# Attention, token routing and expert layers on one core: later weight loads, one engine for the bf16 copies, a new order for the attention part

## The chip, the core and the metric

One core of a Trainium2 chip runs the whole program. The metric is the device time of one execution in microseconds (us), lower is better; the median of several runs is quoted. The engines are PE (TensorE matmul; PEld is its weight load), DVE (VectorE), ACT (ScalarE), POOL (GpSimd) and SP (SyncE, which here only issues DMAs). Each engine runs its own instructions in the order in which they were written, and waits on semaphores for the others.

## The reference

Two stages. The first is a decaying linear attention over q, k, v of shape (4 batches, 8 heads, 768 positions, 64 channels); the second gives each of the 3072 tokens to one of 8 experts, 384 tokens to each, by a greedy pass over the sorted gate logits, and runs the expert's two matmuls.

```python
intra = np.einsum('bhic,bhjc->bhij', qb, kb) * Dmask[None]
intra = np.einsum('bhij,bhjd->bhid', intra, vb)
inter = np.einsum('bhid,bhde->bhie', qb * lam_pow[None], kv_state)
out[:, :, sl] = intra + inter
...
logits = x @ w_gate
order = np.argsort(-flat)
...
h = np.maximum(x[mask] @ w1[e], 0.0)
out[mask] = h @ w2[e]
```

## The kernel before

**Attention** works in 24 groups of 128 positions (6 per batch, all 8 heads together). A group is a chain of about thirty named steps, listed in `_Attn.OPS` with an engine, a planned duration and the steps that they follow. For group g:

- SP loads q, k and v (`ldq`, `ldk`, `ldv`, L1092, 256 KB each, in rows of 256 bytes) into tiles of a pool with seven buffers per name, so that the load of group g waits until group g-7 has been used up.
- POOL or DVE splits k into a high and a low half in place (`klo`, L1098, tile kf); POOL scales v (`vs`, L1113), ACT rounds it (`vh`), POOL takes the rest (`vl`, L1124).
- PE turns q and k (L1129), forms the scores S (L1166); ACT copies them out (`sph`, L1173), DVE takes the low half (`spl`, L1179), POOL zeroes what lies above the diagonal (`mk`, the mask, L1183, tile sp), and PE multiplies with v (`in0`, `in1`, L1206) and with the running state (`inter`, L1194). `state`, `sth`, `stl` carry the state on.
- DVE scales the result (`xs`, L1215). `xb` (L1224 on ACT, L1226 on DVE) makes a bf16 copy, in one of four buffers, and SP stores it to x_dram (`stx`, L1229). PE, ACT and DVE turn and split x (`Tx`, `xh`, `xl`, L1243) and form the gate logits (`gate`, `lg`, L1256).

**Routing and experts.** When all logits are there, DVE and PE rank them (L156 to L404). Pieces of that ranking for the first groups, and constants that POOL makes with iotas (L50, L39), are planned into the last part of the attention. Then POOL gathers the tokens of an expert from x_dram (L657), PE runs the two matmuls (L688, L701), POOL scatters the rows out (L707). The sixteen weight tensors (w1 and w2 of eight experts, 2 MB of f32 read and 1 MB of bf16 written each) are loaded by DMAs that POOL issues (`load_w`, L639, tile w): nine are planned into the attention part (the steps `lw`), seven follow among the gathers.

**What sets the order.** `_Plan.emit` plays all steps through once, with the planned durations and a fixed latency per engine, and always takes the step that can begin first; among those within 0.05 us of each other the lowest number `OFF[name] + g * PERIOD` wins. The kernel is then written out in that order, engine by engine. The plan leaves no wait behind: at run time an engine waits only for the data or the buffer that an instruction needs. A weight load in the attention part needs neither, so POOL issues it as soon as it comes to it in its queue.

Of the kernel before, what the change touches and what calls it, by code (L numbers as in the profile page):

```python
# [17 lines left out]
ACT = mybir.ActivationFunctionType  # L18
# [790 lines left out]
def _check_and_mend(ctx, tc, L, router, moe, dram, fi):  # L809
    fv = tc.nc.values_load(fi, min_val=0, max_val=1)  # L810
    moe.free = False
    with tc.If(fv > 0):
        with ExitStack() as fctx:
            _exact_path(fctx, tc, L, router, moe, dram)
# [225 lines left out]
class _Attn:  # L1040

    PERIOD = 4.65
    OFF = dict(S=54.69, Tk=24.2, Tq=49.21, Tx=-82.61, gate=99.21, in0=35.81, in1=1.68, inter=74.69, kT=111.17, klo=26.02, ldk=11.31, ldq=7.1, ldv=7.57, lg=-21.29, mk=-54.22, qh=-5.75, ql=31.77, sph=96.51, spl=-4.24, state=12.87, sth=69.68, stl=10.78, stx=59.94, vh=-1.2, vl=94.76, vs=-6.84, xb=69.71, xh=15.09, xl=21.76, xs=38.18)

    def __init__(self, ctx, tc, q, k, v, lam, w_gate, identf, logits, x_dram):
        nc = tc.nc
# [230 lines left out]
    def stl(self, g):  # L1277
# [5 lines left out]
        ("ldq", "SP", 1.16, None, "Tq-7"),  # L1283
        ("ldk", "SP", 1.16, None, "state-7 Tk-7"),
        ("ldv", "SP", 1.16, None, "vs-7"),
        ("klo", "Pool", 1.18, None, "ldk"),
        ("vs", "Pool", 1.10, None, "ldv vl-2"),
        ("vh", "ACT", 0.64, None, "vs state-4 in0-4 in1-4"),
        ("vl", "Pool", 1.18, None, "vh state-4 in0-4 in1-4"),
        ("Tq", "PE", 0.42, None, "ldq ql-1"),  # L1290
        ("qh", "ACT", 0.60, None, "Tq S-3 inter-3"),
        ("ql", "DVE", 0.69, None, "qh S-3 inter-3"),
# [1 line left out]
        ("kT", "ACT", 0.62, None, "Tk S-2"),  # L1294
        ("S", "PE", 0.68, None, "kT ql spl-1"),
        ("sph", "ACT", 1.02, None, "S in0-2 in1-2"),
        ("spl", "DVE", 1.22, None, "sph"),
        ("mk", "Pool", 1.35, None, "spl"),
# [14 lines left out]
    )  # L1313

    def engine(self, name, g, eng, dur):
        if name == "xb":
            return (("ACT", 0.63), ("DVE", 0.40))[g % 2]
        if name == "klo" and g % 3 == 2:
            return "DVE", 0.78
        return eng, dur  # L1320

    def plan(self, plan, extra):
# [8 lines left out]
        for g in range(24):  # L1331
            for name, eng, dur, when, deps in self.OPS:
# [12 lines left out]
                if name in ("klo", "xb"):  # L1345
                    f = lambda g, f=f, eng=eng: f(g, getattr(self.nc, en[eng]))
                plan.op(name, g, eng, dur, lambda f=f, g=g: f(g), dd + extra.get((name, g), []),
                        self.OFF[name] + g * self.PERIOD)


@with_exitstack
def kernel(
    ctx: ExitStack,
    tc: tile.TileContext,
    q: bass.AP,
    k: bass.AP,
    v: bass.AP,
    lam: bass.AP,
    moe_w_gate: bass.AP,
    moe_w1: bass.AP,  # L1360
    moe_w2: bass.AP,
    out: bass.AP,
):
    nc = tc.nc
    P = 128
    E = mybir.EngineType
    const = ctx.enter_context(tc.tile_pool(name="const", bufs=1))
    dram = ctx.enter_context(tc.tile_pool(name="dram", bufs=1, space=bass.MemoryType.DRAM))
    identf = const.tile([P, P], F32, name="identf")
    identb = const.tile([P, P], BF16, name="identb")  # L1370
    logits = const.tile([P, 24, 8], F32, name="logits")
    x_dram = dram.tile([3072, 512], BF16, name="x_dram")
    router = _Router(ctx, tc, identf, identb)
    moe = _Moe(ctx, tc, identb, x_dram, moe_w1, moe_w2, out, 10)
    with ExitStack() as actx, tc.manual_schedule(
            engines={E.PE, E.Pool, E.DVE, E.Activation, E.SP}):
        attn = _Attn(actx, tc, q, k, v, lam, moe_w_gate, identf, logits, x_dram)
        attn.consts()
        plan = _Plan()
        extra = {}  # L1380
        router.plan(plan, attn, logits, extra)
        for m in range(9):
            plan.op("lw", m, "Pool", 0.9, lambda m=m: moe.load_w(m),
                    [("mk", min(15 + m, 23)), ("lw", m - 1)], 0)
        attn.plan(plan, extra)
        plan.emit()
    moe.open(ctx)
    fi = _route_and_moe(ctx, tc, logits, router, moe, range(9, 16))
    _check_and_mend(ctx, tc, logits, router, moe, dram, fi)
# [31 lines left out]
```

## Time and profile before

| | |
|---|---|
| median of 3 runs | 310.71 us (307.69 to 315.24) |
| the profiled execution's own time | 310.75 us |
| its span, first to last instruction | 308.9 us |
| mean granted clock of PE | 0.895 of full speed |
| busy, share of the span | PE 78%, DVE 60%, ACT 49%, POOL 57% |
| HBM read and written | 55.60 MB and 9.44 MB |

The span is 1.85 us shorter than the execution's own time; what lies around it is not seen by the profile. A share of busy time is a mean over stages that have different limits, so the prediction reads stages. In the rows below a time begins with the start in us from the beginning of the span, then the duration; a bracket at the end is the idle time of the engine before the instruction and what ended it. In a row of the stages stand, after the stretch and its length, the busy us of PE, PEld, DVE, ACT and POOL (with the number of instructions), the granted PE clock, the busy share of the 16 DMA engines (which can go a little over 1) and what they moved in GB/s. In a row by lines stand the count, the busy us and the mean ns of one, and the idle time before.

### The profile page before, as it was taken

The page shows a single profiled execution, that of the slowest core. Times are in us where ns is not written, and L with a number is a line of the kernel's source. Part 1 is how long each engine was busy: PE and PEld are TensorE (multiplying, and loading weights), DVE is VectorE, ACT ScalarE, POOL GpSimd, SP SyncE. Part 2 cuts the span into 40 slices and gives each one's busy share as a digit, 9 for nine tenths or more (in the row PEclk, how much of TensorE's full clock was granted, in tenths as well). Part 3 has the DMA queues.
Part 4 walks back from the last instruction along what each step waited for, and adds up shares of the span by engine and source line. Part 5 has one row for each costly group of instructions (what it writes and reads, how often), then busy time and mean ns, then how long its engine had stood idle before and what let it go on. Part 6 is the DMA issues. An engine that isn't in the chain of part 4 may idle for free.

```text
span 308.9 us, 8631 instructions
## 1 busy us (share of the span) xinstructions
PE 240.8 (78%) x3512; PEld 193.7 (63%) x3525; DVE 185.7 (60%) x560; ACT 151.3 (49%) x261; POOL 177.4 (57%) x184
## 2 busy tenths in 40 slices
PE   1698988898998149985339986999787999799980
PEld 0678976787897048874237784666455676567750
DVE  0479997979999147999974756577854770000000
ACT  4489776768885226852000001444334445456650
POOL 1799979698993088989650064854262246334220
PEclk9999999979999758997555685899999999999997
DMA  7998998999999969999930019899996113212111
GB/s 138 219 217 181 202 206 195 227 231 233 224 217 175 217 143 165 219 215 222 218 61 0 2 52 145 154 211 227 243 228 243 71 68 114 104 61 102 70 72 40
DMA packets 94671, 48.90 MB, mean 158 GB/s; under 512 B 76960, under 2 KB 88224, under 8 KB 94624
## 3 DMA queue, kind: packets, MB, share of 16 engines
q0 software_dynamic: 15616, 26.22, 40.3%
q1 hardware_dynamic: 79008, 22.05, 34.8%
q8 instruction: 30, 0.49, 0.7%
q14 instruction: 17, 0.14, 0.2%
HBM read 55.60 MB, written 9.44 MB: 211 GB/s over the span
## 4 chain that ended last, share of the span: by engine, by line
PE 30%; DVE 17%; issue 17%; DMA 14%; POOL 13%; ACT 4%; SPq 1%; POOLq 0%; ACTq 0%; DVEq 0%
DMA out_dram<-oe,perm 6%; PE p L688 5%; DMA w<-in_moe_w_dram 4%; PE p L701 4%; DVE sp L1179 4%; PE spare L272 4%; PE S L1166 3%; POOL sp L1183 3%; PE XL L1206 2%; POOL out_dram L707 2%; PE stp L1267 2%; POOL kf L1098 2%; DVE xb L1226 2%; PE KT L1129 2%; POOL vs L1113 2%
## 5 line engine op out<-in xcount | busy, mean ns | idle before, releaser
L688 PE MATMUL p<-xeT,w 128*128 128x256 bf16 (+1 forms) x512 | 50.1, 252 | 6.8 <-ACT xeT L675 2.4
L688 PEld LDWEIGHTS <-w 128*128 128x128 bf16 x512 | 40.5, 100 | 15.4 <-issue 8.6
L707 POOL DMA_INDIRECT out_dram<-oe,perm x24 | 24.0, 999 | 43.6 <-ACT oe L706 32.8
L657 POOL DMA_INDIRECT xe<-x_dram,perm x24 | 25.4, 1058 | 40.6 <-DVE B L387 20.7
L701 PE MATMUL p<-w,hT 128*128 128x512 bf16 x179 | 43.7, 379 | 0.8
L693 ACT ACTIVATE hT<-p 128x512 bf16<-128x512 f32 (+1 forms) x64 | 30.9, 492 | 19.5 <-PE p L688 13.7
L675 ACT COPY xeT<-pt 128x1024 bf16<-128x1024 bf16 (+1 forms) x16 | 12.8, 800 | 43.4 <-PE pt L671 41.0
L1179 DVE TENSOR_TENSOR sp<-S,sp 128x1024 f16<-128x1024 f32 x24 | 31.9, 1330 | 2.8 <-ACT sp L1173 2.4
L1183 POOL TENSOR_SCALAR_AFFINE_SELECT sp<-sp 128x1024 f32<-128x1024 f32 x24 | 27.0, 1127 | 7.6 <-DVE sp L1179 6.9
L1113 POOL TENSOR_TENSOR vs<-vf,lamneg 128x512 f32<-128x512 f32 x24 | 27.5, 1149 | 6.2 <-DMA vf<-in_v_dram 6.1
L1124 POOL TENSOR_TENSOR vl<-vs,vh 128x512 bf16<-128x512 f32 x24 | 28.2, 1182 | 2.1 <-ACT vh L1119 2.1
L706 ACT COPY oe<-p 128x512 f32<-128x512 f32 x24 | 14.0, 588 | 31.1 <-PE p L701 21.2
L1173 ACT ACTIVATE sp<-S 128x1024 f32<-128x1024 f32 x24 | 24.7, 1030 | 7.9 <-PE S L1166 7.0
L701 PEld LDWEIGHTS <-hT 128*128 128x128 bf16 x192 | 17.0, 97 | 17.9 <-issue 1.8
L1098 POOL TENSOR_TENSOR kf<-kf 128x512 f16<-128x512 f32 x16 | 17.0, 1064 | 17.9 <-DMA kf<-in_k_dram 17.9
L1206 PE MATMUL XL<-vh,sp 128*128 128x64 bf16 x384 | 23.5, 199 | 1.6 <-POOL sp L1183 0.8
L1166 PE MATMUL S<-qh,kT 64*128 64x128 f16 x384 | 21.1, 221 | 4.4 <-DVE sp L1179 4.1
L1267 PE MATMUL stp<-vl,kf 128*128 128x128 bf16 x80 | 16.0, 232 | 10.9 <-POOL vl L1124 10.9
L1129 PE MATMUL QT<-identf,qf 128*128 128x128 f32 x96 | 16.6, 299 | 9.3 <-DMA qf<-in_q_dram 5.0
L1206 PEld LDWEIGHTS <-sp 128*128 128x128 bf16 (+1 forms) x576 | 21.8, 102 | 2.9 <-POOL sp L1183 2.2
L1267 PEld LDWEIGHTS <-kf 128*128 128x128 bf16 (+1 forms) x240 | 16.1, 105 | 11.8 <-issue 11.0
L1166 PEld LDWEIGHTS <-kT 64*128 64x128 bf16 (+1 forms) x576 | 17.5, 96 | 7.9 <-issue 6.9
(255 smaller groups left out, 569.6 us busy)
## 6 DMA issues: line engine op xcount, KB each, us to landing
w<-in_moe_w_dram POOLq DMA_DIRECT2D x16, 1024.0 KB
qf<-in_q_dram SPq DMA_DIRECT2D x24, 256.0 KB, 5.2
kf<-in_k_dram SPq DMA_DIRECT2D x24, 256.0 KB, 4.8
vf<-in_v_dram SPq DMA_DIRECT2D x24, 256.0 KB, 5.4
x_dram<-xb SPq DMA_DIRECT2D x24, 128.0 KB, 4.7
xe<-x_dram,perm POOLq DMA_INDIRECT x24
out_dram<-oe,perm POOLq DMA_INDIRECT x24
lam_sb<-in_lam_dram SPq DMA_DIRECT2D x1, 4.0 KB, 2.9
```

What stands on the lines that cost most here:

```text
L657: nc.gpsimd.indirect_dma_start(out=xe[:, c, :], out_offset=None, in_=self.x_dram, in_offset=bass.IndirectOffsetOnAxis(ap=pm, axis=0), boun ...
L688: nc.tensor.matmul(p1[:, f, 0:n, :], self.w1t[e][:, kc, fc * P : (fc + 1) * P], j["xeT"][:, kc, 0:n, :], start=(kc == 0), stop=(kc == 3), ...
L693: nc.scalar.activation(hT[:, fp, :, 0:n, :], p1[:, :, 0:n, :], ACT.Relu)
L701: nc.tensor.matmul(p2, j["hT"][:, kc // 2, kc % 2, c, :], self.w2t[e][:, kc, :], start=(kc == 0), stop=(kc == 7))
L707: sc = nc.gpsimd.indirect_dma_start(out=self.out, out_offset=bass.IndirectOffsetOnAxis(ap=j["perms"][c], axis=0), in_=oe, in_offset=None, ...
L1113: self.nc.gpsimd.tensor_tensor(d["vs"], d["v"], self.lamneg[:, g % 6, :, None].to_broadcast([128, 8, 64]), OP.mult)
L1124: self.nc.gpsimd.tensor_tensor(d["vl"], d["vs"], d["vh"], OP.subtract)
L1166: self.nc.tensor.matmul(S[:, a, hp, :], kk[r, hp, :], qq[r, hp, :], start=(i == 0), stop=(i == 2))
L1179: self.nc.vector.tensor_tensor(lo, d["S"].rearrange("p a c i -> p (a c i)"), hi, OP.subtract)
L1183: self.nc.gpsimd.affine_select(out=sf, in_=sf, compare_op=OP.is_ge, fill=0.0, base=0, pattern=[[0, 8], [1, 128]], channel_multiplier=-1)
L1206: self.nc.tensor.matmul(d["XL"][:, a, hp, :], ss[:, a, hp, :], vv[:, 2 * hp + a, :], start=(first and hp == 0 and i == 0), stop=(i == 2), ...
L1267: self.nc.tensor.matmul(self.stp[:, hp, :], kk[:, hp, :], vv[:, hs, :].rearrange("p h d -> p (h d)"), start=(g % 6 == 0 and hp == 0 and i ...
```

## The change

Four things are changed.

1. A weight load in the plan now follows the last loads of q, k and v (group 23) as well as the mask 15 + m.
2. All 24 bf16 copies `xb` are on ACT; before, the 12 odd groups were on DVE.
3. DVE keeps `klo` of groups 4, 9, 14 and 19; before, it had groups 2, 5, 8, 11, 14, 17, 20 and 23. POOL so has 20 of the 24 instead of 16.
4. Planned durations of five steps are set anew, and the table `OFF` is another one.

```diff
@@ class _Attn
-    OFF = dict(S=54.69, Tk=24.2, Tq=49.21, Tx=-82.61, gate=99.21, in0=35.81, in1=1.68, inter=74.69, kT=111.17, klo=26.02, ldk=11.31, ldq=7.1, ldv=7.57, lg=-21.29, mk=-54.22, qh=-5.75, ql=31.77, sph=96.51, spl=-4.24, state=12.87, sth=69.68, stl=10.78, stx=59.94, vh=-1.2, vl=94.76, vs=-6.84, xb=69.71, xh=15.09, xl=21.76, xs=38.18)
+    OFF = dict(S=38.76, Tk=-14.89, Tq=147.97, Tx=-2.41, gate=2.43, in0=170.45, in1=-148.02, inter=-167.53, kT=141.1, klo=52.88, ldk=36.69, ldq=34.47, ldv=38.97, lg=-259.14, mk=-45.12, qh=27.26, ql=58.61, sph=117.65, spl=65.52, state=205.19, sth=37.97, stl=-17.43, stx=-83.47, vh=74.3, vl=-25.62, vs=110.96, xb=281.9, xh=-1.86, xl=-37.54, xs=47.27)
...
-        ("klo", "Pool", 1.18, None, "ldk"),
+        ("klo", "Pool", 1.06, None, "ldk"),
...
-        ("vl", "Pool", 1.18, None, "vh state-4 in0-4 in1-4"),
+        ("vl", "Pool", 1.17, None, "vh state-4 in0-4 in1-4"),
...
-        ("spl", "DVE", 1.22, None, "sph"),
-        ("mk", "Pool", 1.35, None, "spl"),
+        ("spl", "DVE", 1.33, None, "sph"),
+        ("mk", "Pool", 1.12, None, "spl"),
...
-        ("xb", None, 0.63, None, "xs stx-4"),
+        ("xb", "ACT", 0.62, None, "xs stx-4"),
...
     def engine(self, name, g, eng, dur):
-        if name == "xb":
-            return (("ACT", 0.63), ("DVE", 0.40))[g % 2]
-        if name == "klo" and g % 3 == 2:
-            return "DVE", 0.78
+        if name == "klo" and g % 5 == 4:
+            return "DVE", 0.95
         return eng, dur
...
-                    [("mk", min(15 + m, 23)), ("lw", m - 1)], 0)
+                    [("ldq", 23), ("ldk", 23), ("ldv", 23), ("mk", 15 + m), ("lw", m - 1)], 0)
```

POOL's queue around its first weight loads, before (kf is `klo`, sp the mask, w a weight load; the mask behind w_0_70 is that of group 16, the `klo` behind w_0_71 that of group 22):

```order
L1113 TENSOR_TENSOR vs<-vf,lamneg 128x512
L639 DMA w_0_70<-in_moe_w_dram 128x4x1024
L1183 AFFINE_SELECT sp<-sp 128x1024
L1098 TENSOR_TENSOR kf<-kf 128x512
L639 DMA w_0_71<-in_moe_w_dram 128x8x512
L1098 TENSOR_TENSOR kf<-kf 128x512
L1124 TENSOR_TENSOR vl<-vs,vh 128x512 x2
L1183 AFFINE_SELECT sp<-sp 128x1024
```

The same place after (the first `klo` is group 22's, the second group 23's; the first mask is group 17's):

```order
L1098 TENSOR_TENSOR kf<-kf 128x512
L1183 AFFINE_SELECT sp<-sp 128x1024
L1124 TENSOR_TENSOR vl<-vs,vh 128x512
L639 DMA w_0_70<-in_moe_w_dram 128x4x1024
L1098 TENSOR_TENSOR kf<-kf 128x512
L639 DMA w_0_71<-in_moe_w_dram 128x8x512
L1183 AFFINE_SELECT sp<-sp 128x1024
L639 DMA w_1_72<-in_moe_w_dram 128x4x1024
L1113 TENSOR_TENSOR vs<-vf,lamneg 128x512
L639 DMA w_1_73<-in_moe_w_dram 128x8x512
L1183 AFFINE_SELECT sp<-sp 128x1024
```

The first weight load has moved from behind mask 15 to behind mask 17 and `klo` 22; only `klo` 23 stands behind it, and the loads follow each other more closely.

SP's queue near its end, before (group 22's last two loads, then those of group 23 and stores of x):

```order
L1092 DMA vf<-in_v_dram 128x8x64
L1229 DMA x_dram<-xb 128x512
L1092 DMA kf<-in_k_dram 128x8x64
L1092 DMA qf<-in_q_dram 128x8x64
L1092 DMA vf<-in_v_dram 128x8x64
L1229 DMA x_dram<-xb 128x512
L1092 DMA kf<-in_k_dram 128x8x64
L1229 DMA x_dram<-xb 128x512 x11
```

The same queue after, around its only run of three stores (the loads ahead are q and k of group 17):

```order
L1092 DMA qf<-in_q_dram 128x8x64
L1092 DMA kf<-in_k_dram 128x8x64
L1229 DMA x_dram<-xb 128x512 x3
L1092 DMA vf<-in_v_dram 128x8x64
L1092 DMA qf<-in_q_dram 128x8x64
L1092 DMA kf<-in_k_dram 128x8x64
```

Thirteen stores stand ahead of the last load in both programs; before, they come one to a group from group 11 on, after, they stand earlier and less evenly, the first behind sixteen loads.

DVE's queue at the end of the attention, before (L1179 is `spl` of group 23; L178 to L188 are pieces of the ranking):

```order
L1179 TENSOR_TENSOR sp<-S,sp 128x1024
L178 TENSOR_SCALAR dg<-identf,m_3305 3x3
L1226 CAST xb<-xs 128x512
L1243 TENSOR_TENSOR xl<-XT,xh 128x512
L1215 TENSOR_TENSOR xs<-XL,lampow 128x2x4x64
L1256 TENSOR_REDUCE logits<-XT 128x8
L1280 TENSOR_TENSOR stl<-stp,sth 128x512
L185 COPY mb<-mb_ps 128x3
L1226 CAST xb<-xs 128x512
L188 TENSOR_SCALAR rg<-mb 128x2
```

The same place after:

```order
L178 TENSOR_SCALAR dg<-identf,m_3333 3x3
L1179 TENSOR_TENSOR sp<-S,sp 128x1024
L1243 TENSOR_TENSOR xl<-XT,xh 128x512
L1215 TENSOR_TENSOR xs<-XL,lampow 128x2x4x64
L1256 TENSOR_REDUCE logits<-XT 128x8
L1280 TENSOR_TENSOR stl<-stp,sth 128x512
L185 COPY mb<-mb_ps 128x3
L188 TENSOR_SCALAR rg<-mb 128x2
L191 SCALAR_TENSOR_TENSOR lo<-rg,mb 128x2
```

The copies are gone from DVE, and the ranking's small steps stand directly behind the attention's. From the gathers on, the order of every engine is the same in both programs.

## Rows read from the trace of the kernel before

**Rows 1.** Busy time by stages, core 0.

```profile
65.00:92.00 27.00, 25.25 (x573) 23.41 (x572) 24.77 (x40) 22.66 (x38) 25.01 (x23) 0.98 1.04 225
92.00:112.00 20.00, 8.28 (x189) 6.89 (x187) 8.79 (x15) 7.39 (x13) 6.14 (x7) 0.80 1.11 206
112.00:139.00 27.00, 23.93 (x510) 21.76 (x510) 23.86 (x38) 17.89 (x30) 23.86 (x24) 0.90 0.98 176
139.00:152.00 13.00, 6.07 (x90) 5.06 (x86) 12.63 (x32) 2.30 (x4) 10.63 (x20) 0.72 1.18 219
152.00:180.00 28.00, 21.11 (x174) 16.52 (x174) 18.36 (x75) 0.00 (x0) 6.72 (x9) 0.58 0.19 37
```

**Rows 2.** POOL in order of time: masks, weight load, `klo`, iotas, first gather.

```profile
42.04 1.09 POOL L1183 TENSOR_SCALAR_AFFINE_SELECT sp<-sp 128x1024 f32<-128x1024 f32 x1 [0.69 <-DVE logits L1256]
...
50.28 1.08 POOL L1183 TENSOR_SCALAR_AFFINE_SELECT sp<-sp 128x1024 f32<-128x1024 f32 x1
...
71.03 1.09 POOL L1183 TENSOR_SCALAR_AFFINE_SELECT sp<-sp 128x1024 f32<-128x1024 f32 x1 [1.56 <-DVE sp L1179]
...
91.34 1.00 POOL L639 DMA_DIRECT2D w<-in_moe_w_dram  x1
92.87 1.09 POOL L1183 TENSOR_SCALAR_AFFINE_SELECT sp<-sp 128x1024 f32<-128x1024 f32 x1 [0.53 <-DVE sp L1179]
...
109.18 1.03 POOL L1098 TENSOR_TENSOR kf<-kf 128x512 f16<-128x512 f32 x1 [13.33 <-DMA kf<-in_k_dram]
...
112.39 1.08 POOL L1183 TENSOR_SCALAR_AFFINE_SELECT sp<-sp 128x1024 f32<-128x1024 f32 x1
...
138.49 1.09 POOL L1183 TENSOR_SCALAR_AFFINE_SELECT sp<-sp 128x1024 f32<-128x1024 f32 x1
...
141.18 3.58 POOL L50 IOTA i_kt<- 128x768 bf16 x4
...
179.77 1.60 POOL L657 DMA_INDIRECT xe<-x_dram,perm  x1 [20.70 <-DVE B L387]
```

**Rows 3.** SP's last loads in order of time, and how long loads took to land.

```profile
93.63 0.46 SPq L1092 DMA_DIRECT2D kf<-in_k_dram  x1
94.14 8.11 SPq L1092 DMA_DIRECT2D qf<-in_q_dram  x1
...
108.86 0.39 SPq L1092 DMA_DIRECT2D kf<-in_k_dram  x1
...
DMA to landing us min/median/max: 3.6/5.2/16.1
```

**Rows 4.** DMA queues from 88 to 110 us: packets, MB, share of 16 engines.

```profile
q1 hardware_dynamic: 8373, 2.38, 57.7%
q0 software_dynamic: 1568, 2.10, 55.3%
```

**Rows 5.** DVE in order of time at the end of the attention.

```profile
138.06 1.54 DVE L178 TENSOR_SCALAR dg<-identf,m 3x3 f32<-3x3 f32 x1
...
141.86 3.99 DVE L1226 CAST xb<-xs 128x512 bf16<-128x512 f32 x1
...
148.44 1.43 DVE L1226 CAST xb<-xs 128x512 bf16<-128x512 f32 x1
...
151.52 0.17 DVE L1256 TENSOR_REDUCE logits<-XT 128x8 f32<-128x16 f32 x1 [0.15 <-PE XT L1252]
```

**Rows 6.** Groups of instructions by line: copies, v's scaling, `klo`, weight loads.

```profile
L1113 POOL TENSOR_TENSOR vs<-vf,lamneg 128x512 f32<-128x512 f32 x24 | 27.5, 1149 | 6.2 <-DMA vf<-in_v_dram 6.1
...
L1098 POOL TENSOR_TENSOR kf<-kf 128x512 f16<-128x512 f32 x16 | 17.0, 1064 | 17.9 <-DMA kf<-in_k_dram 17.9
...
L639 POOL DMA_DIRECT2D w<-in_moe_w_dram x16 | 14.2, 891 | 2.9 <-DMA w<-in_moe_w_dram 2.9
...
L1226 DVE CAST xb<-xs 128x512 bf16<-128x512 f32 x12 | 13.4, 1116 | 0.0
...
L1224 ACT CAST xb<-xs 128x512 bf16<-128x512 f32 x12 | 7.5, 623 | 11.9 <-issue 7.0 <-DMA x_dram<-xb 3.3 <-DVE xs L1215 1.7
```

## The prediction

> **What bounds the kernel now.** I read the stages first, then POOL in order of time, then what SP and the DMA queues did where POOL stood still.
>
> The stages [rows 1] show a hole. From 65 to 92 us PE, DVE and POOL are each busy for about 25 of 27 us, and the DMA engines move 225 GB/s: everything is near its limit at once. From 92 to 112 us no engine is busy for half of the time, but the DMA share is 1.11. The DMAs work, and not on what the engines wait for.
>
> POOL in order of time [rows 2] says where. The masks of groups 11 and 16 start at 71.03 and 92.87, five groups apart, so a group takes 4.37 us. The next mask, group 17's, starts at 112.39, 19.52 us later. Just before, at 91.34, POOL issued the first weight load; then `klo` of group 22 waited 13.33 us for its k. That k had been issued at 93.63 [rows 3], so it took over 15 us to land where the median load takes 5.2; the issue of the next q alone held SP for 8.11 us, and the last k went out only at 108.86. Between 88 and 110 us the two queues had nearly equal shares of the DMA engines, 55.3% for the weights and 57.7% for loads and stores [rows 4]. Two weight tensors, not needed before the gathers at 179.77 [rows 2], took half of the service from the last few loads, needed at once.
>
> By the Trainium skill, page "DMA: Bandwidth & Descriptors", section "Queues, rings and completion order", each DMA engine takes turns between the queues that have work, a packet at a time. The nearly equal shares agree with that.
>
> The second place is the end of the attention. From the last mask at 138.49 [rows 2] to the last logits at 151.52 [rows 5] 13.03 us pass, DVE is busy for 12.63 of 13 us [rows 1], and two bf16 copies take 3.99 and 1.43 us there [rows 5], while POOL runs its iotas from 141.18 [rows 2].
>
> **The change part by part.** The sum is made against the profiled execution, 310.75 us, which is the median of the runs shown (310.71) for all purposes.
>
> *Weight loads later: -15.2.* In the new order the first weight load stands behind mask 17 and `klo` 22. When POOL reaches it, k of group 22 has landed, and of 72 loads only the last few can be in flight. If the pitch of 4.37 holds for one more group, mask 17 starts at 92.87 + 4.37 = 97.24 instead of 112.39: 15.15 us. What is late next is the pitch itself. It can't fall far: up to k of group 22 there are 68 loads of 262 kB and 12 stores of 131 kB, 19.4 MB, at 225 GB/s 86 us; with some 2 us of start, 5.2 for landing and 1.06 for `klo` [rows 6] mask 17 can't start before about 94.5, a further 2.7 at best. On the other side, the old order once lost a group's time to such waiting: masks at 42.04 and 50.28 are 8.24 apart, 3.87 over the pitch. Two such gaps of the new order's own would cost 7.7. I take 0 between -2.7 and +7.7, as the pitch of five full groups is the nearest row.
>
> *`xb` to ACT, `klo` to POOL: 0 until mask 17.* DVE loses twelve copies of 1.12 us mean and ACT gains twelve of 0.62 [rows 6]; ACT is busy for 22.66 of 27 us between 65 and 92 [rows 1] and takes in 0.3 us more per group. POOL gains four `klo` of 1.06, three of them before mask 17, and its 25.01 of 27 has room for them. With the DMAs as near their limit as the engines, I give DVE's relief no value here; it lies inside the bound of -2.7. If the cover on POOL is gone, the three cost 3.2, inside the 7.7.
>
> *POOL from mask 17 to mask 23: +1.0.* This took 138.49 - 112.39 = 26.10 us. POOL now has there one `vs` less (1.15), two weight loads more (2 x 0.89), one `klo` (1.06, [rows 6]) and one iota (a quarter of 3.58, [rows 2]): +2.6. Its instructions are short of the stage by 27 - 23.86 = 3.1 us [rows 1], waits for DVE, which now has fewer things to do. So between 0 (all of it fills waits) and +2.6; I take +1.0, nearer to the cover. Behind each issue stand the next mask and with it PE's `in0`; that is why two issues more count at all.
>
> *The end of the attention: -4.2.* The two copies, 5.4 us, leave DVE's chain. But the small steps behind them now meet the iotas. L178 shows what that costs: it lasts 1.54 us, from 138.06 to 139.60, and the mask that POOL began at 138.49 ends at 139.58. I give back 1.2. Bounds: -5.4 (nothing given back) and -1.4 (the next step inherits the whole wait of 3.99).
>
> By the Trainium skill, page "SBUF — State Buffer", section "Who interferes with whom", certain DVE instructions and POOL's share a port pair that one holds for its whole instruction, and the other waits. By that rule a step would wait for one iota, 0.9 us, and the term would be -4.5; the row of the copy, which lasted through all four iotas, would make it -1.4. Between them the trace does not decide.
>
> *After the last logits: 0.* The order is the same from the gathers on, so gathers, expert matmuls and the later weight loads move as one block. The point to watch is whether the nine early weights have landed by then. The first leaves at about 97.24 + 2.3 = 99.5; with three loads and eleven stores 11.7 MB are then left, 53 us at 219 GB/s or 66 at 176 [rows 1], so they end between 153 and 166. The first gather, 179.77 before [rows 2], would come at 161.4: between 8 us early and 4.6 late. I take 0, bounds 0 and +4.6. The DMA share of 0.19 from 152 to 180 [rows 1] is the slack that this uses up.
>
> Sum: -15.15 + 1.0 - 4.2 = -18.35, so 310.75 - 18.35 = 292.4 us. All bounds on the good side give -15.15 - 2.7 - 5.4 = -23.25, or 287.5; all on the bad side but the gather's -15.15 + 7.7 + 2.6 - 1.4 = -6.3, or 304.5.
>
> **The rivals.**
>
> *The new order has waits of its own.* Two gaps as that between 42.04 and 50.28 come back: 292.4 + 7.7 = 300.1. For it: every `klo` runs five groups ahead of its mask in POOL's queue, so a late k stops all of POOL. Against it: DVE, the other full engine, is relieved.
>
> *It doesn't do what it says.* Nothing in the program makes POOL wait for the last loads; the plan only places the issue. If q, k and v of group 23 still queue when the first weight load goes out, `klo` 23, right behind it, waits 13.3 again: 292.4 + 13.3 = 305.7, no change that can be told (2%, 6.2 us, is about what a measurement of this kernel can tell from none). Against it: at most three loads are left, 3.5 us alone at 225 GB/s.
>
> By the rule on taking turns, those three would last twice as long, 7 us instead of 3.5, and the sum would be 3.5 higher; no row before shows so few loads against the weights.
>
> *Slower: stores hold up the loads.* The thirteen stores ahead of SP's last load now stand in eleven places among loads from the sixteenth on, and each waits for a copy by ACT. A place costs nothing while earlier loads are still in flight (5.2 us), and up to a group's pitch, 4.37, when they run dry. From five of the eleven places on the gain is gone (5 x 4.37 = 21.9 > 18.35); six give 292.4 + 26.2 = 318.6. For it: SP is one queue, and three stores stand in a row. Against it: the seven buffers hold groups in advance, and the copies can run well before a store is reached.
>
> **How the numbers follow.** My forecast has 0.69, all of it faster by over 2% (under 304.5). Waits of the new order's own: 0.17, of which 0.15 still faster and 0.02 within 2%. No effect: 0.09, within. Held-up loads: 0.05, of which 0.03 slower by over 2% and 0.02 within. That makes 0.84 faster, 0.13 within, 0.03 slower. The range goes from 286 (the best sum, less some 1 us for a piece of the ranking, L229, which now stands ahead of the last logits) to 303, which holds the second case and leaves out the third and fourth and the tails, some 2 in 10.
>
> **What would show it.** Right: mask 17 starts at 94 to 100 us, no `klo` waits over 3 us for k after 90 us, the first weight load goes out near 99, mask 23 starts near 124, the last logits come within 10 us of it, and the first gather is at about 161. The granted clock, 0.80 in the hole [rows 1], stays near 0.98 there. The sum is wrong in its first term if mask 17 comes after 104; in the tail if a step on DVE lasts over 2 us beside the iotas; in the last if the gather's rows land after the weights and PE stands still for them. If mask pitches over 8 us recur before 90 us while SP waits for a copy, the fourth case holds.

## The result and the profile after

The changed kernel takes 293.88 us (median of 4 runs, 293.82 to 297.44), beside 310.35 us for the kernel before on the same chip (4 runs, 307.69 to 315.24). The ratio is 0.9525, 95% interval 0.9418 to 0.9631: faster. The ratios, here and below, compare the means of those runs that were in the faster of the chip's two states, and so are not the quotients of the medians. The forecast was 292.4 us with a range of 286 to 303. The profiled execution took 293.82 us, its span is 292.0 us; PE's mean granted clock is 0.912.

The stages of the changed kernel, core 0, with the columns of [rows 1]; the bounds are those of its own masks:

```profile
65.00:92.00 27.00, 25.57 (x588) 23.30 (x584) 24.36 (x37) 23.43 (x40) 23.41 (x23) 1.00 0.99 217
92.00:112.00 20.00, 17.62 (x410) 15.81 (x407) 15.72 (x26) 16.85 (x29) 19.92 (x21) 1.00 0.97 182
112.00:124.00 12.00, 10.09 (x215) 8.99 (x215) 9.58 (x18) 8.98 (x16) 10.60 (x11) 0.86 1.16 226
124.00:136.00 12.00, 5.65 (x105) 4.81 (x101) 11.37 (x29) 3.06 (x6) 9.42 (x18) 0.80 1.18 216
...
152.00:162.00 10.00, 9.30 (x80) 7.32 (x79) 6.13 (x19) 0.00 (x0) 0.00 (x0) 0.83 0.08 15
```

The hole is closed. From 92 to 112 us POOL is busy for 19.92 of 20 us where it was busy for 6.14 [rows 1], PE for 17.62 instead of 8.28, and the clock is 1.00 instead of 0.80. The last row shows the DMA engines idle just before the first gather: the nine early weights have landed.

POOL of the changed kernel in order of time, what answers to [rows 2]: the masks of groups 16, 17 and 23, the first weight load, the last `klo`, iotas, the first gather:

```profile
93.45 1.09 POOL L1183 TENSOR_SCALAR_AFFINE_SELECT sp<-sp 128x1024 f32<-128x1024 f32 x1
...
97.63 1.10 POOL L1183 TENSOR_SCALAR_AFFINE_SELECT sp<-sp 128x1024 f32<-128x1024 f32 x1
...
99.79 1.00 POOL L639 DMA_DIRECT2D w<-in_moe_w_dram  x1
100.82 1.05 POOL L1098 TENSOR_TENSOR kf<-kf 128x512 f16<-128x512 f32 x1
...
124.00 1.09 POOL L1183 TENSOR_SCALAR_AFFINE_SELECT sp<-sp 128x1024 f32<-128x1024 f32 x1
...
126.72 1.81 POOL L50 IOTA i_kt<- 128x768 bf16 x2
128.47 0.86 POOL L39 IOTA i_j<- 128x696 bf16 x1
...
162.20 1.60 POOL L657 DMA_INDIRECT xe<-x_dram,perm  x1 [20.33 <-DVE B L387]
```

Mask 17 starts at 97.63 us, 14.76 earlier than before. The `klo` behind the first weight load, group 23's, has no bracket: it waited for nothing. From 100 to 102 us the queue of loads and stores passed a single packet, so no load of q, k or v was left for the weights to hold up. All loads of q, k and v now land within 6.0 us, where one took 16.1 [rows 3]:

```profile
DMA to landing us min/median/max: 3.6/5.1/6.0
```

DVE of the changed kernel at the end of the attention, what answers to [rows 5]:

```profile
126.03 0.15 DVE L185 COPY mb<-mb_ps 128x3 f32<-128x3 f32 x1
126.21 3.16 DVE L188 TENSOR_SCALAR rg<-mb 128x2 f32<-128x2 f32 x1
...
131.85 1.31 DVE L225 TENSOR_SCALAR y<-r_zv 128x10 f32<-128x10 f32 x1
...
135.34 0.17 DVE L1256 TENSOR_REDUCE logits<-XT 128x8 f32<-128x16 f32 x1 [0.21 <-PE XT L1252]
```

The copies are gone, but a step on two elements per partition, `rg`, lasts 3.16 us beside POOL's iotas, and L225 lasts 1.31 us beside a memset that POOL runs from 131.74 to 133.13. Before, the copies of 3.99 and 1.43 us [rows 5] stood there, the second beside the same memset (148.22 to 149.60). By spans the change divides as follows (mask 17, mask 23, last logits, first gather and end; us):

| stretch | before | after | difference |
|---|---|---|---|
| start to mask 17 | 112.39 | 97.63 | -14.76 |
| mask 17 to mask 23 | 26.10 | 26.37 | +0.27 |
| mask 23 to the last logits | 13.03 | 11.34 | -1.69 |
| last logits to the first gather | 28.25 | 26.86 | -1.39 |
| first gather to the end | 129.13 | 129.80 | +0.67 |
| span | 308.9 | 292.0 | -16.90 |

### The profile page after: what moved, and what is told of

The parts are those of the page before. It is cut to its first block, busy times and chain, and to the rows that moved or that the text cites. A ratio compares the mean times of both kernels' runs of the same rounds, so it can differ in the third digit from the quotient of the medians.

```text
span 292.0 us, 8617 instructions
## 1 busy us (share of the span) xinstructions
PE 239.5 (82%) x3512; PEld 192.0 (66%) x3525; DVE 173.5 (59%) x544; ACT 157.7 (54%) x273; POOL 176.6 (60%) x188
## 4 chain that ended last, share of the span: by engine, by line
PE 32%; DMA 19%; DVE 13%; issue 12%; POOL 12%; SPq 5%; ACT 4%; POOLq 0%; ACTq 0%; DVEq 0%
DMA out_dram<-oe,perm 11%; DMA kf<-in_k_dram 8%; PE p L688 5%; SPq L1092 4%; PE p L701 4%; PE spare L272 4%; PE S L1166 3%; POOL xe L657 2%; POOL vl L1124 2%; PE XL L1206 2%; POOL out_dram L707 2%; PE stp L1267 2%; POOL kf L1098 2%; POOL sp L1183 2%; PE XT L1129 2%
## 5 line engine op out<-in xcount | busy, mean ns | idle before, releaser
L693 ACT ACTIVATE hT<-p 128x512 bf16<-128x512 f32 (+1 forms) x64 | 31.1, 491 | 19.3 <-PE p L688 13.3
L1179 DVE TENSOR_TENSOR sp<-S,sp 128x1024 f16<-128x1024 f32 x24 | 32.2, 1342 | 4.7 <-ACT sp L1173 4.4
L1098 POOL TENSOR_TENSOR kf<-kf 128x512 f16<-128x512 f32 x20 | 21.0, 1049 | 11.5 <-DMA kf<-in_k_dram 11.5
L1183 POOL TENSOR_SCALAR_AFFINE_SELECT sp<-sp 128x1024 f32<-128x1024 f32 x24 | 26.2, 1092 | 2.2 <-DVE sp L1179 2.2
L1206 PE MATMUL XL<-vh,sp 128*128 128x64 bf16 x384 | 24.1, 195 | 2.6 <-POOL sp L1183 2.2
L1113 POOL TENSOR_TENSOR vs<-vf,lamneg 128x512 f32<-128x512 f32 x24 | 25.4, 1064 | 0.4 <-DMA vf<-in_v_dram 0.4
L1166 PE MATMUL S<-qh,kT 64*128 64x128 f16 x384 | 22.4, 231 | 0.3 <-DVE sp L1179 0.3
L1206 PE MATMUL XL<-vl,sp 128*128 128x64 bf16 x192 | 21.5, 195 | 0.0
L1129 PE MATMUL KT<-identf,kf 128*128 128x128 f32 x96 | 16.1, 293 | 5.5 <-POOL kf L1098 4.0
L1166 PEld LDWEIGHTS <-kT 64*128 64x128 bf16 (+1 forms) x576 | 18.2, 101 | 3.2 <-issue 1.9
```

What stands on the lines that cost most here:

```text
L693: nc.scalar.activation(hT[:, fp, :, 0:n, :], p1[:, :, 0:n, :], ACT.Relu)
L1098: eng.tensor_tensor(lo, d["k"].rearrange("p h d -> p (h d)"), hi, OP.subtract)
L1129: self.nc.tensor.transpose(ps[:, hp, :], src(hp), self.identf)
L1166: self.nc.tensor.matmul(S[:, a, hp, :], kk[r, hp, :], qq[r, hp, :], start=(i == 0), stop=(i == 2))
L1179: self.nc.vector.tensor_tensor(lo, d["S"].rearrange("p a c i -> p (a c i)"), hi, OP.subtract)
L1183: self.nc.gpsimd.affine_select(out=sf, in_=sf, compare_op=OP.is_ge, fill=0.0, base=0, pattern=[[0, 8], [1, 128]], channel_multiplier=-1)
```

## The experiments

The theory is the prediction's: weight loads that run beside the last loads of k opened the hole, and planning them later closed it. The rival is that the relief of DVE, `klo` on POOL and the new table of the order did it. The runs came in three groups (e1 to e4, e5 to e8, e9 to e12); the kernel before took 312.94, 311.7 and 311.04 us beside them, and the ratios are to its runs of the same group.

**The old order, two weight loads later (e1).** The order, the copies and `klo` are those of before; only these two issues move on POOL.

```diff
+        mask = attn.mask
+        def mask_then_load(g):
+            mask(g)
+            if g == 17:
+                moe.load_w(0)
+                moe.load_w(1)
+        attn.mask = mask_then_load
...
-            plan.op("lw", m, "Pool", 0.9, lambda m=m: moe.load_w(m),
+            plan.op("lw", m, "Pool", 0.9, lambda m=m: moe.load_w(m) if m > 1 else None,
```

> The kernel before, with its order as it was, but the first two weight loads are issued right behind the mask of group 17 instead of around the mask of group 16. If the loads of q and k were late because the weights took turns with them on the DMA engines, no byte of a weight is under way when k of group 22 is fetched: its klo waits under 3 us instead of 13.3, mask 17 starts at 96 to 99 us instead of 112.4, and the total is 295 to 299 us. Rival, the new order and the relief of DVE made the gain: the hole closes by less than 3 us and the total stays over 306 us.

Measured: 301.07 us, ratio 0.9683 (0.9595 to 0.9772). POOL of this kernel in order of time: masks 16 and 17, and the two `klo` ahead of mask 17:

```profile
91.35 1.09 POOL L1183 TENSOR_SCALAR_AFFINE_SELECT sp<-sp 128x1024 f32<-128x1024 f32 x1 [1.45 <-DVE sp L1179]
93.89 1.36 POOL L1098 TENSOR_TENSOR kf<-kf 128x512 f16<-128x512 f32 x1 [1.45 <-DMA kf<-in_k_dram]
98.11 1.04 POOL L1098 TENSOR_TENSOR kf<-kf 128x512 f16<-128x512 f32 x1 [2.86 <-DMA kf<-in_k_dram]
...
101.32 1.10 POOL L1183 TENSOR_SCALAR_AFFINE_SELECT sp<-sp 128x1024 f32<-128x1024 f32 x1
```

The wait of 13.33 us [rows 2] is 2.86, and mask 17 comes 11.07 us earlier with nothing else changed. So the weights made the wait. But mask 17 and the total are each 2 us past the range expected, and 9.97 us lie between masks 16 and 17: with the weights gone this order still waits for k, 1.45 and 2.86 us.

**Only the second load later (e2).** As e1, with the first weight load left at its old place.

```diff
             if g == 17:
-                moe.load_w(0)
                 moe.load_w(1)
```

> The kernel before, with only the second of these two weight loads moved behind mask 17; the first goes out at its old place, at about 91 us. If the queues share the engines by turns, one load of 2 MB read is enough: in the hole of 20 us the DMA engines moved 176 GB/s, 3.5 MB, of which the weights' half is some 1.8 MB, so the second load was hardly under way then. Mask 17 starts at 107 to 112 us and the total is 305 to 310 us. Rival, what counts is how many weight bytes are issued: half of the delay, mask 17 at about 105 us, and a total of about 303 us.

Measured: 305.18 us, ratio 0.9801 (0.9686 to 0.9916). POOL of this kernel, `klo` of group 22 and mask 17:

```profile
102.75 1.04 POOL L1098 TENSOR_TENSOR kf<-kf 128x512 f16<-128x512 f32 x1 [8.79 <-DMA kf<-in_k_dram]
...
105.96 1.09 POOL L1183 TENSOR_SCALAR_AFFINE_SELECT sp<-sp 128x1024 f32<-128x1024 f32 x1
```

Mask 17 is just under the range of the first theory and near the rival's 105. My reading of the shares as halves was wrong. So was the premise that the second load was hardly under way: by 110 us 2.10 MB of weights had gone through [rows 4], two loads of 1.05 (and 176 GB/s is the rate of the stage behind the hole, which itself has 206 [rows 1]). The DMA queues over four microseconds of the hole say how (q0 carries the weights that POOL issues, q1 SP's loads and stores; packets, MB, share of 16 engines). The kernel before, 96 to 100 us:

```profile
q0 software_dynamic: 376, 0.69, 92.1%
q1 hardware_dynamic: 381, 0.10, 18.4%
```

The kernel before, 100 to 104 us:

```profile
q0 software_dynamic: 587, 0.60, 88.8%
q1 hardware_dynamic: 591, 0.21, 31.7%
```

The kernel of e1, without weights under way, 96 to 100 us:

```profile
q1 hardware_dynamic: 3418, 0.96, 116.9%
```

The queues pass equal numbers of packets, 376 to 381 and 587 to 591, not equal time. The weights' packets are of 0.69 MB / 376 = 1.8 KB and then 1.0 KB, those of the loads and stores of 0.26 to 0.36 KB, so the weights take five and then three times the service. The counts are as equal elsewhere while both queues have work: 164 to 156 from 96 to 98 us in e2, 305 to 299 from 105 to 107 us in e3. The 55.3% and 57.7% of [rows 4] were a mean over a stretch whose first part held no weights. Loads that pass 3418 packets in 4 us when alone pass 381 beside the weights, so they wait for most of the weights' own service. That is 0.553 x 22 = 12.2 us for the two loads of [rows 4], and for the one of e2, from 88 to 106 us:

```profile
q0 software_dynamic: 528, 1.05, 33.2%
```

0.332 x 18 = 6.0 us. Measured: mask 17 at 101.32 with neither, 105.96 with the first (+4.64), 112.39 with both (another 6.43). So a service of 12.2 us made a delay of 11.07, and one of 6.0 a delay of 4.64. The two loads have equal bytes and nearly equal service, so these times don't tell a delay by service from the rival's delay by bytes; that the queues take turns rests on the packet counts.

By the Trainium skill, page "DMA: Bandwidth & Descriptors", section "Queues, rings and completion order", an engine goes round the queues a packet at a time. The counts of these rows agree, if what the profile counts as a packet (here one row of a tile: 1.05 MB in 528 packets are 2 KB each) is the packet of the page, which no run here shows. It was I who had read equal shares of time into the rule.

**The new order with the old rule (e3).**

```diff
-                    [("ldq", 23), ("ldk", 23), ("ldv", 23), ("mk", 15 + m), ("lw", m - 1)], 0)
+                    [("mk", min(15 + m, 23)), ("lw", m - 1)], 0)
```

> The changed kernel with the old rule for the weight loads: the first goes out behind mask 16, a klo earlier than k of group 23 is there, with the rest of the order nearly the same. If the rule made the gain, a wait of 6 to 13 us for k comes back on POOL and the total is 300 to 307 us. Rival, the new order brings the loads in early enough to stand the weights beside them: the total stays at 296 us or below.

Measured: 307.87 us, ratio 0.9823 (0.9673 to 0.9973). POOL of this kernel in order of time (an execution of 309.88 us):

```profile
92.35 1.00 POOL L639 DMA_DIRECT2D w<-in_moe_w_dram  x1
...
106.52 1.04 POOL L1098 TENSOR_TENSOR kf<-kf 128x512 f16<-128x512 f32 x1 [6.54 <-DMA kf<-in_k_dram]
...
116.65 1.03 POOL L1098 TENSOR_TENSOR kf<-kf 128x512 f16<-128x512 f32 x1 [8.37 <-DMA kf<-in_k_dram]
```

The wait is back, 6.54 and 8.37 us for the last two k, within the 6 to 13 us expected; the total is just past its range of 300 to 307. By the ratios all else that the change does is worth 1.8% as long as the old rule stands (interval 0.3% to 3.3%, 1 to 10 us); with the new rule the same program gains 4.8%, another 9 us.

**The old order with the new rule (e4).**

```diff
-                    [("mk", min(15 + m, 23)), ("lw", m - 1)], 0)
+                    [("ldq", 23), ("ldk", 23), ("ldv", 23), ("mk", 15 + m), ("lw", m - 1)], 0)
```

> The kernel before with the new rule for the weight loads alone; bf16 copies, klo and the table of the order are those of before. If the rule made the gain, mask 17 starts at 96 to 99 us, the tail of the attention keeps its two bf16 copies on DVE and its 13 us, and the total is 296 to 300 us, 2 to 5 us over the changed kernel. Rival, the order searched anew made it: a total over 306 us.

Measured: 302.47 us, ratio 0.9715 (0.9600 to 0.9830), a little over the range. Mask 17 starts at 104.40, not at 96 to 99; the plan, played through anew, put a `vs`, another `vl` and the first weight load ahead of it. By the ratios the rule alone thus gives 2.9% (e4), and later weight loads alone 3.2% (e1), of the 4.8 to 5.2% that the whole change gives (e11 for the latter): 9 to 10 us of 15 to 16.

**The parts of the rest, on e1 and on the changed kernel (e5, e7, e8).** Copies or `klo` change their engine when the instructions are written, the plan stays as it is.

```diff
 e5, on e1
-                    f = lambda g, f=f, eng=eng: f(g, getattr(self.nc, en[eng]))
+                    f = lambda g, f=f, e=("ACT" if name == "xb" else eng): f(g, getattr(self.nc, en[e]))
 e7, on the changed kernel
-                    f = lambda g, f=f, eng=eng: f(g, getattr(self.nc, en[eng]))
+                    f = lambda g, f=f, e=("DVE" if name == "xb" and g % 2 else eng): f(g, getattr(self.nc, en[e]))
 e8, on e1
-                    f = lambda g, f=f, eng=eng: f(g, getattr(self.nc, en[eng]))
+                    f = lambda g, f=f, e=(eng if name == "xb" else "DVE" if g % 5 == 4 else "Pool"): f(g, getattr(self.nc, en[e]))
```

> The kernel before with the first two weight loads behind mask 17 (301.1 us) and besides with all 24 bf16 copies on ACT, at the same places of the order. If the relief of DVE is worth nothing while the DMA engines are full, as the prediction has it, mask 17 stays at 100 to 102 us, and only the tail gains: the small step behind the copies takes over the wait beside the iotas, 12.8 us from mask 23 to the last logits become about 11.3, total 299 to 300 us. Rival, DVE's relief is what the new order gains before mask 17: it starts at 97 to 99 us, total 295 to 297 us.

> The changed kernel with the twelve odd bf16 copies back on DVE, at the same places of the order. If the copies count only in the tail, mask 17 stays at 97 to 98.5 us, the tail grows from 11.3 to 12.5 to 14 us, total 295 to 297 us. Rival, ACT's copies are what lets the order keep its pitch: mask 17 at 100 to 103 us, total 298 to 301 us.

> The kernel before with the first two weight loads behind mask 17 (301.1 us) and with klo divided as in the changed kernel, 20 on POOL and 4 on DVE, at the same places of the order. If, as the prediction has it, POOL's gaps take the four klo, mask 17 stays at 100 to 103 us and the total at 300 to 303 us. Rival, klo on POOL is part of the gain before mask 17: it starts at 97 to 99 us, total 297 to 298 us.

| | us | ratio (95%) | mask 17 | mask 17 to 23 | to the last logits |
|---|---|---|---|---|---|
| e1 | 301.07 | 0.9683 (0.9595-0.9772) | 101.32 | 26.57 | 12.76 |
| e5, copies on ACT | 297.85 | 0.9570 (0.9496-0.9644) | 101.00 | 26.02 | 12.30 |
| e8, `klo` as after | 301.03 | 0.9702 (0.9636-0.9769) | 100.84 | 27.04 | 12.76 |
| changed kernel | 293.88 | 0.9525 (0.9418-0.9631) | 97.63 | 26.37 | 11.34 |
| e7, odd copies on DVE | 298.91 | 0.9596 (0.9512-0.9680) | 99.47 | 28.90 | 11.86 |

`klo` is not seen to be worth anything (e8). Neither part moves mask 17 beyond what it moves from profile to profile, which e11 below shows. e5 is lower than expected, but its stretch up to the last logits is 12.30 us, where about 11.3 was expected; its trace gains only 1.3 us up to the last logits, and its interval overlaps that of e1. e7 was expected to lose in the tail; its total is the rival's, but not by the rival's way: mask 17 is where the changed kernel has it too (99.44 in e11), and 2.5 us are lost between masks 17 and 23. DVE of e7 in order of time, a copy beside POOL and one later on:

```profile
119.92 4.56 DVE L1226 CAST xb<-xs 128x512 bf16<-128x512 f32 x1
...
126.54 0.40 DVE L1226 CAST xb<-xs 128x512 bf16<-128x512 f32 x1
```

POOL of e7 in the same stretch:

```profile
119.03 1.17 POOL L1124 TENSOR_TENSOR vl<-vs,vh 128x512 bf16<-128x512 f32 x1
120.17 1.03 POOL L1113 TENSOR_TENSOR vs<-vf,lamneg 128x512 f32<-128x512 f32 x1
121.16 1.08 POOL L1183 TENSOR_SCALAR_AFFINE_SELECT sp<-sp 128x1024 f32<-128x1024 f32 x1
122.22 1.14 POOL L1124 TENSOR_TENSOR vl<-vs,vh 128x512 bf16<-128x512 f32 x1
123.32 0.94 POOL L639 DMA_DIRECT2D w<-in_moe_w_dram  x1
...
128.37 1.09 POOL L1183 TENSOR_SCALAR_AFFINE_SELECT sp<-sp 128x1024 f32<-128x1024 f32 x1 [3.08 <-DVE sp L1179]
```

A copy of the same shape takes 0.40 us later; this one lasts 4.56, beside four compute steps of POOL without a gap, and mask 23 then waits 3.08 us for `spl`, which stands behind the copies on DVE.

**The iotas in front of the first `klo` (e6).** On the changed kernel; POOL waits 4.7 us there for its first k.

```diff
-        pc, dc = self.pool_constants(), self.dve_constants()
+        pc, dc = self.pool_constants(), self.dve_constants(); [next(pc) for _ in range(5)]
...
-            plan.op("pc", i, "Pool", d, lambda: next(pc), [("pc", i - 1), ("mk", i // 2)], 1e6 + i)
+            plan.op("pc", i, "Pool", d, lambda i=i: next(pc) if i > 4 else None, [("pc", i - 1), ("mk", i // 2)], 1e6 + i)
```

> The changed kernel with the identity and the four iotas i_kt issued before the first klo, where POOL waits 4.7 us for its k, instead of among the last masks and loads. If rg lasted 3.16 us because POOL ran these iotas beside it, rg falls under 0.5 us, the last logits come 2 to 3 us nearer to mask 23, and the total is 291 to 292 us. Rival, the remaining iotas of POOL move up and stretch another step of DVE, or PE is what ends the tail: less than 1 us, 293 to 294.5 us. Second rival: the opening is late by the iotas, and the total is above 295 us.

Measured: 291.68 us, ratio 0.9367 (0.9282 to 0.9453). DVE of e6 in order of time:

```profile
127.04 0.15 DVE L185 COPY mb<-mb_ps 128x3 f32<-128x3 f32 x1
127.23 0.55 DVE L188 TENSOR_SCALAR rg<-mb 128x2 f32<-128x2 f32 x1
...
133.86 0.17 DVE L1256 TENSOR_REDUCE logits<-XT 128x8 f32<-128x16 f32 x1 [0.21 <-PE XT L1252]
```

`rg` falls from 3.16 to 0.55 us, and from mask 23 (125.03) to the last logits 8.83 us pass instead of 11.34. The opening isn't late: mask 0 starts at 13.84 against 13.87.

**The place of k among the loads (e9, e10).** In the new order 67 loads and 12 stores (19.14 MB) are issued ahead of k of group 22, in the old one 68 and 12 (19.40 MB): v comes behind k instead of ahead of it. Both kernels exchange k and v from group 8 on, e9 on e1 and e10 on the changed kernel.

```diff
-            fn["ld" + n] = lambda g, n=n: self.load(g, n) if g else None
+            fn["ld" + n] = lambda g, n=n: self.load(g, dict(q="q", k="v", v="k")[n] if g > 7 else n) if g else None
```

> The kernel before with the first two weight loads behind mask 17 (301.1 us), and from group 8 on k is loaded where v was and v where k was, so that k of group 22 has 262 kB of v and a store of 131 kB less ahead of it on SP. If what is left of the gap to the changed kernel (mask 17 at 101.3 against 97.6) is the place of k in the stream of loads, k of group 22 lands some 1.8 us earlier (0.39 MB at 214 GB/s) and mask 17 starts at 99 to 100.5 us, total 298 to 300.5 us. Rival, SP then waits for the buffer of k, which is freed later than that of v, and all loads behind it are late: mask 17 at 101 us or later, total 301 to 305 us.

> The changed kernel with the same exchange: from group 8 on v is loaded where k was and k where v was, so that k of group 22 comes one load later on SP. If the place of k in the stream counts, mask 17 starts 1 to 2 us later, at 98.6 to 100 us, and the total is 295 to 297 us. Rival, the order has slack for one load: mask 17 within 0.6 us of 97.6, total 293 to 294.5 us.

Measured: e9 300.10 us, ratio 0.9743 (0.9640 to 0.9845), mask 17 at 99.93 (e1 101.32); e10 296.72 us, ratio 0.9605 (0.9496 to 0.9714), mask 17 at 100.45 (changed kernel 97.63). Both move the way that the place of k would move them, and each lies some 1 us outside the profiles without the exchange (100.84 to 101.32 in the old order, 97.63 to 99.47 in the new one). With one profile each, and with 1.8 us between profiles of one and the same kernel (e11), that is a hint and not shown.

**The changed kernel and e6 once more, side by side (e11, e12).**

> The changed kernel once more, beside the next run on the same chip: 292.5 to 295 us. Mask 17, mask 23 and the last logits within 1 us of 97.6, 124.0 and 135.3; what these move by is what a row of one profile can tell.

> The changed kernel with the identity and the four iotas in front of the first klo, once more, beside the changed kernel on the same chip. If the 2.2 us between 293.9 and 291.7 are its own, it is 1.5 to 3 us below the changed kernel here too, with 8.5 to 9.5 us from mask 23 to the last logits against 11 to 11.8. Rival, that was the spread between two chips: less than 1 us.

Measured: 292.84 us, ratio 0.9479 (0.9400 to 0.9558), and 292.91 us, ratio 0.9449 (0.9362 to 0.9536). As times they are the same; the rival holds. In the traces the tail agrees with e6: from mask 23 to the last logits 11.33 us in e11 (`rg` 3.69 us) and 8.84 in e12 (`rg` 0.28). But mask 17 of e11 starts at 99.44 and mask 23 at 126.55, 1.8 and 2.6 later than in the first profile of the same kernel; that was more than the 1 us I expected (each profiled execution was the longest of its six, 297.31 and 294.77 us). A gain of 2.5 us in one stretch is no more than what mask 23 moves by from profile to profile. So early iotas are shown to shorten the tail, and not shown to shorten the kernel.

## Why the prediction was right, and where not

*The weight loads, -15.2.* Measured -14.76 up to mask 17. The mechanism is shown by both of its sides: taken away from the old order, the wait goes (e1); put back into the new order, it returns (e3). The size came out for a reason that was only in part the one given, and in part by luck. "If the pitch of 4.37 holds for one more group" fails in the old order, where 9.97 us lie between masks 16 and 17 even without weights. There the rule gives 11.1. The rest is the new order's: mask 17 starts at 97.63, 98.96, 99.47, 99.44 and 99.26 in its five profiles with the new rule and k in its place (the changed kernel, e6, e7, e11, e12), mean 98.95, against 101.05 for the old order without early weights (e1, e5, e8). That is 2.1 us in the mean and 3.7 in the profile that was compared, which has the earliest mask 17 of the five: by their mean the term measures -13.4. What in the order does it, the place of k or the fuller queue of the stretches before, is left open: e9 and e10 lean to the former, and do not show it.

*What is late next.* The prediction put mask 17 at 94.5 at best, because the loads alone need 86 us. Something of this bound is seen in e1: POOL waits there for k at a DMA share of 0.96 to 1.02 (65 to 97 us), though mask 17 stands 6.8 us above the 94.5. In the changed kernel it waits 1.14 and 1.77 us at 91.46 and 87.10 and no longer at 96.64.

*`xb` and `klo`: 0 until mask 17.* Held: 101.00 and 100.84 against 101.32.

*POOL from mask 17 to mask 23, +1.0.* Measured +0.27, and +1.0 in e11 (27.11 us), inside the bounds of 0 and 2.6.

*The tail, -4.2.* This is the term that was mis-sized: -1.69, close to the bad bound of -1.4. The step that failed is "I give back 1.2", taken from L178, which met one mask. The row to take was the copy's own, 3.99 us, which outlasted the four iotas by 1.1 us (to 145.85 against 144.76) and met the next one, `i_j`, too: the next step of that kind, `rg`, took over its wait. The second copy's 1.43 us passed in the same way to L225, 1.31. By the prediction's own signs this term failed: a step on DVE lasted over 2 us, and the last logits came 11.34 us after mask 23, not within 10. In e6 and e12, without the iotas beside it, `rg` loses its wait and the stretch 2.5 us. That it is then 13.03 - 8.83 = 4.2 us shorter than before, the very number forecast, is in part chance: another step (L215, 1.21 us) still waits beside the memset, and a piece of the ranking (L229, 0.83 us) has come into the stretch.

*After the last logits, 0.* -1.39 up to the gather, +0.67 from there on. That L229 now stands ahead of the last logits was named as some 1 us for the range and belonged into the sum. The weights had landed in time: DMA share 0.08 from 152 to 162 us, the gather at 162.20 for the 161.4 of the forecast.

*The sum.* -18.35 forecast, -16.90 measured in the span: the tail's 2.5 too little, the ranking's 1.4 too much, the rest within 0.8 each and nearly cancelling.

*The rivals.* Waits of the new order's own: its largest pitch before mask 17 is 6.63 us (47.25 to 53.88), none over 8. In e11 one of 7.91 comes (82.76 to 90.67, with a wait of 3.67 us for k): waits of the order's own exist, of less than the 3.87 us over the pitch that the rival had twice. No effect: `klo` 23 waited for nothing; its price was not measured as named, 13.3 us for one k; in e3, with two k behind the weights, the two waits make 14.9. Stores that hold up the loads: in the changed kernel no store ahead of a load held SP for over 2.1 us, and the loads landed within 6.0 us. The 7 us that the prediction made of three loads by the rule on turns took equal times for equal turns; by the packet counts of the hole, with up to five times the service for the weights, it would have been more.

## What to carry to other kernels

Compare queues by packets, not by bytes or by a share averaged over a stretch. Here a queue of packets of 1 to 2 KB starved one of 0.26 KB packets beside it, and bulk loads that nobody needed yet cost the last small loads most of their own service time (11.07 of 12.2 us, 4.64 of 6.0). When a slow instruction is taken off an engine, ask whether it was slow by itself or because of what ran beside it; if the latter, price the next instruction of its kind with the full wait. Run each part of a change by itself before giving it the credit, even when the sum came out right.

## What the runs showed of the hardware

Two queues with work pass packets one for one: 376 to 381 and 587 to 591 in 4 us, at 92.1% to 18.4% and 88.8% to 31.7% of the engines' service. That the equal shares of the longer stretch were an accident of its bounds I had not expected.

A copy on DVE does not wait for one instruction of POOL only. In e7 it began at 119.92 and ended at 124.48, and in that time POOL ran the last part of one `vl`, a `vs`, a mask, another `vl` and a DMA issue back to back; later a copy of the same shape took 0.40 us. In the changed kernel `rg` lasted 3.16 us beside iotas and 0.55 in e6, where they had been moved away; DVE's two-input steps `xl` and `xs`, which read one input from PSUM, took their usual 0.69 us beside iotas (130.27 and 130.94 us in the changed kernel). By the Trainium skill, page "SBUF — State Buffer", section "Who interferes with whom", the engine that comes first has the shared ports for its whole instruction. The rows go further: the waiting instruction can stay behind several more of POOL's that follow without a gap.
